# Zero matmuls ahead of a step: in the step's own PSUM tile, or in a spare tile first

## The chip, the cores and the metric

The kernel runs on one core of a Trainium2 chip. The metric is the device time of one execution in microseconds; lower is better. Three timed executions of the kernel before took 207.27, 207.66 and 207.92 us.

## The reference

A linear-attention recurrence (RWKV6) over 4 batches, 8 heads, 768 tokens and a head dimension of 48, followed by a gated feed-forward block (SwiGLU) on the 3072 tokens of width 384, with a hidden width of 1536. Inputs and output are float32.

```python
for t in range(S):
    cur = np.einsum('bhd,bhe->bhde', u[None] * kt, vt)
    y[:, :, t] = np.einsum('bhd,bhde->bhe', rt, state + cur)
    state = wt[:, :, :, None] * state + np.einsum('bhd,bhe->bhde', kt, vt)
...
xn = x / np.sqrt(np.mean(x * x, axis=-1, keepdims=True) + 1e-06) * rms_g
g = xn @ w_gate
out = (g * (1.0 / (1.0 + np.exp(-g))) * (xn @ w_val)) @ w_out
```

## The kernel before

The recurrence is worked in chunks of 128 tokens. There are six superblocks `n`, each with the chunks of the four batches `j`, and a step of the kernel carries its block as (n, j). For each chunk the kernel takes the logarithm of w (`ln`), sums it along the tokens by matmuls with a triangular mask (`cs_mm`), takes exponentials (`exp_r`, `exp_k`), scales r and k (`r_mul`, `k_mul`) and transposes both (`rk_pe` on TensorE and `rk_tr` as the copy out of PSUM, or `rk_tr` as a transposing DMA). It multiplies them (`q_mm`), masks the product (`q_mask_e` on VectorE for the even heads; `q_copy_o` and `q_mask_o` on ScalarE, GpSimd or VectorE for the odd ones), and forms the output of the chunk (`y_mm`) and the new state (`st_mm`, `st_new`). The bonus of the current token is worked on GpSimd and VectorE (`bonus_mul`, `bonus_sum`, `bonus_v`) and added in `x_add`. The normalized rows (`x_sq`, `x_rstd`, `xn_mul`) are transposed (`xn_pe` and `xn_out`, or `xn_tr`). The feed-forward block then runs over twelve column blocks `f` of the hidden width for each superblock: `gate_mm`, `silu`, `val_mm`, `h_mul`, and at last `o_mm`, `o_out` and `out_dma`.

The order of all steps is written out by hand in the table `ORDER`; each engine runs its instructions in that order. Loads and stores of the blocks are issued on the SP queue, the loads of the feed-forward weights on GpSimd's queue.

PSUM has eight tiles, in three rings: `a` and `b` with two each, `q` with four. A step that writes PSUM calls `psum(ring, key, shape)`, which picks the tile of the ring whose last user lies furthest back in the order, and opens a new tile under that tile's name. A new tile under a name waits until the tile before it under that name has been given back, that is until all who wrote or read it are done.

A number behind a colon in `ORDER` (`cs_mm.0.0:2`) asks for that many zero matmuls in front of the step; 17 entries have one, and the numbers add up to 50. The zero matmuls multiply the matrix `zero` (128 x 128, bf16) by itself, 384 columns at a time. Nobody reads what they write; they only keep TensorE working. They stand in `psum` at line 236, and go to a tile of their own under the same name (`spare`), which is given back before the step's tile is opened.

The entries with a number are:

```python
cs_mm.0.0:2 rk_pe.0.0:2 q_mm.0.0:4 q_mm.1.0:2 rk_pe.0.1:2 st_mm.0.1:4 cs_mm.0.3:3 q_mm.0.1:1 rk_pe.1.1:1
q_mm.1.1:7 y_mm.0.1:8 xn_pe.1.0:2 st_mm.1.1:3 rk_pe.0.3:3 val_mm.0.0:4 gate_mm.0.6:1 gate_mm.0.11:1
```

`rk_pe` and `xn_pe` open a bf16 tile, all the others a float32 tile.

Of the kernel before, what the change touches and what calls it, by code (L numbers as in the profile page):

```python
# [9 lines left out]
FP32 = mybir.dt.float32  # L10
BF16 = mybir.dt.bfloat16
# [7 lines left out]
def bc_mid(ap: bass.AP, n: int, axis: int = 1) -> bass.AP:  # L19
    new_ap = [list(x) for x in ap.ap]  # L20
    new_ap.insert(axis, [0, n])
    return dataclasses.replace(ap, ap=new_ap)
# [107 lines left out]
def kernel(  # L130
# [13 lines left out]
    nc = tc.nc  # L144
# [5 lines left out]
    DM = H * D  # L150
# [14 lines left out]
    psP = ctx.enter_context(tc.tile_pool(name="psP", bufs=1, space=bass.MemoryType.PSUM))  # L165
# [49 lines left out]
    steps, ahead = [], []  # L215
    for x in ORDER.split():
        x, _, m = x.partition(":")
# [3 lines left out]
    last_use, at = {}, [0]  # L221
# [6 lines left out]
    def psum(ring, key, shape, dtype=FP32):  # L228
        slots = rings[ring]
        k = min((x for x in range(len(slots)) if slots[x][0] < at[0]), key=lambda x: slots[x])  # L230
        taken[0] += 1
        slots[k] = [last_use.get(key, -1), taken[0]]
        if ahead[at[0]]:
            spare = psP.tile([128, 512], FP32, name="ps_" + ring + "uvxz"[k])
            for _ in range(ahead[at[0]]):
                nc.tensor.matmul(spare[:, 0:DM].rearrange("p (a x) -> p a x", a=3), lhsT=zero, rhs=bc_mid(zero, 3),
                                 start=True, stop=True)
            ahead[at[0]] = 0
        return psP.tile(shape, dtype, name="ps_" + ring + "uvxz"[k])

    table = [None]

# [45 lines left out]
    zero = const.tile([128, 128], BF16)  # L288
    nc.vector.memset(zero, 0.0)
    ident = const.tile([128, 128], BF16)  # L290
# [71 lines left out]
    def warm(n, j):  # L362
        ps = psum("q", ("warm", n, j), [128, DM])
        nc.tensor.matmul(ps.rearrange("p (a x) -> p a x", a=3), lhsT=zero, rhs=bc_mid(zero, 3), start=True, stop=True)

    def u_mm(n, j):
        ps = bank["u", n, j] = psum("q", ("u", n, j), [128, DM])
        nc.tensor.matmul(ps, lhsT=ones_row, rhs=u_row, start=True, stop=True)
# [4 lines left out]
    def g_mm(n, j):  # L373
        ps = bank["gain", n, j] = psum("q", ("gain", n, j), [128, KC])
        nc.tensor.matmul(ps, lhsT=g_row, rhs=i3, start=True, stop=True)
# [334 lines left out]
```

## Time and profile before

| | |
|---|---|
| timed runs | 207.27, 207.66, 207.92 us (median 207.66) |
| profiled execution | 206.26 us, of which 204.5 us are the span of the core's instructions |
| granted TensorE clock in the profile | 1.0 |
| zero matmuls | 50, in 17 groups, from 5.7 to 38.9 us |
| read from and written to memory | 25.96 MB and 4.72 MB |

The page of the profile names each group of instructions by line, engine, operation and tiles (`out<-in`). PE is TensorE's matmuls, PEld its weight loads, DVE VectorE, ACT ScalarE, POOL GpSimd and SP the queue that issues most DMAs. In a timeline a row is its start, its length, the engine, the line and the operation, how many instructions were merged into it (`x4`), and in brackets the idle time of the engine ahead of it with what ended it. The length of a merged row reaches from the first start to the last end. Matmuls overlap in the pipeline, so that the time from one start to the next can be much shorter than the length of one.

### The profile page before, as it was taken

Reading aid. Unit: us, or ns where it says so; the run is one execution under the profiler, and the core shown is the slowest. Engines: PE = TensorE matmul, PEld = TensorE weight load, DVE = VectorE, ACT = ScalarE, POOL = GpSimd, SP = SyncE. Lnnn points to the kernel's source line nnn. Section 1 sums busy time; section 2 is a strip of 40 time slices with the busy share of each in tenths; the row PEclk is TensorE's granted clock in tenths of the full one; section 3 lists DMA queues with packets and bytes.
Section 4 is the critical chain, followed back from the end, with each engine's and each line's share of the span. In section 5 each row is a group of like instructions: output and inputs, shape, how many; then the busy total and the mean of one; then the engine's idle time right before and its main releaser. Section 6 shows DMA issues by size and latency. Waiting matters only on the chain.

```text
span 204.5 us, 4563 instructions
## 1 busy us (share of the span) xinstructions
PE 193.3 (94%) x1657; PEld 120.9 (59%) x1674; DVE 157.8 (77%) x307; ACT 134.8 (66%) x278; POOL 124.4 (61%) x178
## 2 busy tenths in 40 slices
PE   1989999999999999999999998999999999999993
PEld 0355665465568998865556564656555555555562
DVE  5469879699998799998888997997989782225711
ACT  2625984769789666899658985899776683335310
POOL 6488958157849962689849555978699654200000
PEclk9999999999999999999999999999999999999999
DMA  6999999999989999969999999993465003030132
GB/s 148 240 231 221 172 206 203 193 203 180 195 174 227 184 172 239 196 144 148 201 227 203 227 221 158 206 213 77 136 180 106 0 19 101 0 115 0 65 111 98
DMA packets 121567, 32.42 MB, mean 159 GB/s; under 512 B 116420, under 2 KB 120392, under 8 KB 121544
## 3 DMA queue, kind: packets, MB, share of 16 engines
q1 hardware_dynamic: 119504, 28.58, 67.6%
q0 software_dynamic: 2032, 3.54, 9.9%
q8 instruction: 13, 0.21, 0.4%
q14 instruction: 10, 0.08, 0.1%
q10 hardware_dynamic: 8, 0.00, 0.0%
HBM read 25.96 MB, written 4.72 MB: 150 GB/s over the span
## 4 chain that ended last, share of the span: by engine, by line
PE 59%; DMA 4%; ACT 3%; DVE 2%; POOL 1%; SPq 1%; issue 1%; ACTq 0%; DVEq 0%; POOLq 0%
PE ps_qx L656 6%; PE ps_au L613 6%; PE ps_av L613 6%; PE ps_qv L656 6%; PE ps_bu L613 6%; PE ps_bv L613 5%; PE ps_qu L656 5%; PE ps_qz L656 4%; DMA rkT<-rk 2%; PE ps_au L618 2%; PE ps_bu L618 2%; DMA vt<-in_v_dram 2%; PE ps_av L618 2%; PE ps_bv L618 2%; ACT L245 1%
## 5 line engine op out<-in xcount | busy, mean ns | idle before, releaser
L656 PEld LDWEIGHTS <-ht 128*128 128x128 bf16 x300 | 28.1, 98 | 17.5 <-DVE ht L642 1.0
L247 ACT ACTIVATE sg<-ps_av 128x512 bf16<-128x512 f32 x36 | 21.5, 596 | 23.5 <-PE ps_av L613 18.4
L642 DVE TENSOR_TENSOR ht<-ps_bv,sg 128x512 bf16<-128x512 f32 x29 | 19.9, 685 | 13.9 <-PE ps_bv L613 13.0
L247 ACT ACTIVATE sg<-ps_au 128x512 bf16<-128x512 f32 x36 | 21.5, 596 | 11.9 <-PE ps_au L613 8.3
L613 PEld LDWEIGHTS <-wg_sb 128*128 128x128 bf16 x180 | 19.2, 114 | 16.7 <-issue 1.6
L613 PEld LDWEIGHTS <-wv_sb 128*128 128x128 bf16 x180 | 19.1, 114 | 15.9 <-issue 0.8
L471 POOL TENSOR_TENSOR ydiag<-vt,diag 128x384 f32<-128x384 f32 x24 | 20.0, 844 | 10.6 <-DVE diag L466 10.2
L461 POOL TENSOR_TENSOR ruk<-rt,kt 128x384 f32<-128x384 f32 x24 | 24.1, 1003 | 3.5 <-DMA kt<-in_k_dram 2.8
L613 PE MATMUL ps_av<-xnt,wg_sb 128*128 128x512 bf16 x88 | 25.0, 381 | 0.6 <-ACT sg L247 0.2
L642 DVE TENSOR_TENSOR ht<-ps_bu,sg 128x512 bf16<-128x512 f32 x31 | 21.2, 684 | 5.4 <-PE ps_bu L613 3.3
L462 POOL TENSOR_TENSOR ruk<-ruk,u_bc 128x384 f32<-128x384 f32 x24 | 24.0, 1000 | 1.9
L613 PE MATMUL ps_bu<-xnt,wv_sb 128*128 128x512 bf16 x86 | 24.8, 379 | 0.4
L613 PE MATMUL ps_au<-xnt,wg_sb 128*128 128x512 bf16 x87 | 23.6, 380 | 0.1
L613 PE MATMUL ps_bv<-xnt,wv_sb 128*128 128x512 bf16 x82 | 23.2, 380 | 0.3
L455 POOL TENSOR_TENSOR rk<-kt,ek 128x384 bf16<-128x384 f32 x16 | 15.9, 1001 | 9.9 <-ACT ek L247 5.7
L245 ACT ACT_TABLE_LOAD x14 | 18.0, 1283 | 1.9 <-PEq L694 1.6
L656 PE MATMUL ps_qx<-wo_sb,ht 128*128 128x384 bf16 x96 | 17.1, 326 | 0.2 <-DVE ht L642 0.2
L554 ACT ACTIVATE junk<-xb 128x384 bf16<-128x384 f32 x24 | 12.5, 520 | 5.2 <-DVE xb L549 5.1
L567 ACT ACTIVATE xn<-xb,rstd 128x384 bf16<-128x384 f32 x24 | 14.2, 609 | 1.1 <-POOL rstd L563 1.0
L466 DVE TENSOR_REDUCE diag<-ruk 128x8 f32<-128x384 f32 x24 | 12.9, 543 | 1.6 <-POOL ruk L462 1.6
L656 PE MATMUL ps_qv<-wo_sb,ht 128*128 128x384 bf16 (+1 forms) x84 | 13.8, 314 | 0.0
L247 ACT ACTIVATE lw<-wt 128x384 bf16<-128x384 f32 (+1 forms) x20 | 11.5, 582 | 2.3 <-DMA wt<-in_w_dram 2.3
(166 smaller groups left out, 407.3 us busy)
## 6 DMA issues: line engine op xcount, KB each, us to landing
rt<-in_r_dram SPq DMA_DIRECT2D x24, 192.0 KB, 3.9
vt<-in_v_dram SPq DMA_DIRECT2D x24, 192.0 KB, 4.0
kt<-in_k_dram SPq DMA_DIRECT2D x24, 192.0 KB, 4.0
out_dram<-ob SPq DMA_DIRECT2D x23, 192.0 KB, 2.2
wt<-in_w_dram SPq DMA_DIRECT2D x16, 192.0 KB, 4.1
wt<-in_w_dram SPq DMA_DIRECT2D x4, 384.0 KB, 4.2
wo_sb<-in_moe_w_out_dram POOLq DMA_DIRECT2D x3, 384.0 KB, 7.6
wg_sb<-in_moe_w_gate_dram POOLq DMA_DIRECT2D x1, 768.0 KB, 9.2
```

The lines of the kernel that those rows point to most:

```text
L245: nc.scalar.preload_act_table_set(table_name)
L247: return nc.scalar.activation(**kw).ins
L455: eng.tensor_tensor(out=rk[:, n % 2, j, 1, :, 0:D], in0=inp["k", n, j], in1=bank["cs_k", n, j][:, 0:DM].rearrange("p (h d) -> p h d", h=H) ...
L461: nc.gpsimd.tensor_tensor(out=ruk[n, j], in0=inp["r", n, j], in1=inp["k", n, j], op=ALU.mult)
L462: nc.gpsimd.tensor_tensor(out=ruk[n, j], in0=ruk[n, j], in1=u_bc, op=ALU.mult)
L466: nc.vector.tensor_reduce(out=diag[n, j].rearrange("p h o -> p (h o)"), in_=ruk[n, j], axis=mybir.AxisListType.X, op=ALU.add)
L471: nc.gpsimd.tensor_tensor(out=ydiag[n, j], in0=inp["v", n, j], in1=diag[n, j].to_broadcast([128, H, D]), op=ALU.mult)
L567: nc.scalar.activation(out=xn, in_=xb[n, j], func=AF.Copy, scale=rstd[n, j][:, 1:2])
L613: nc.tensor.matmul(ps, lhsT=units(ws, c, f), rhs=x[:, c, :], start=(c == 0), stop=(c == KC - 1))
L618: nc.tensor.matmul(ps[:, i * TS // 2:(i + 1) * TS // 2], lhsT=units(ws, c, f + i), rhs=x[:, c, cols], start=(i == 0 and c == 0), stop=(i = ...
L642: nc.vector.tensor_tensor(out=ht[n][:, f, :], in0=v, in1=sg, op=ALU.mult)
L656: nc.tensor.matmul(ps[:, cols], lhsT=ht[n][:, f, b * L:(b + 1) * L], rhs=wo_sb[:, f, cols], start=(f == 0), stop=(f == FC - 1))
```

## The change

The spare tile is gone. `psum` opens the step's own tile, writes the zero matmuls into that, and hands it to the step, whose first matmul starts a new sum and so overwrites them. In front of a bf16 tile each zero matmul becomes three transposes of `zero`, of 128 columns each. The numbers in `ORDER` and everything else stay. The changed file is four lines longer from there on, so a line L613 of the kernel before is L617 of the changed one.

```diff
         slots[k] = [last_use.get(key, -1), taken[0]]
-        if ahead[at[0]]:
-            spare = psP.tile([128, 512], FP32, name="ps_" + ring + "uvxz"[k])
-            for _ in range(ahead[at[0]]):
-                nc.tensor.matmul(spare[:, 0:DM].rearrange("p (a x) -> p a x", a=3), lhsT=zero, rhs=bc_mid(zero, 3),
+        ps = psP.tile(shape, dtype, name="ps_" + ring + "uvxz"[k])
+        flat = ps if len(shape) == 2 else ps.rearrange("p a b -> p (a b)")
+        for _ in range(ahead[at[0]]):
+            if dtype == BF16:
+                for c in range(3):
+                    nc.tensor.transpose(flat[:, c * 128:(c + 1) * 128], zero, ident)
+            else:
+                nc.tensor.matmul(flat[:, 0:DM].rearrange("p (a x) -> p a x", a=3), lhsT=zero, rhs=bc_mid(zero, 3),
                                  start=True, stop=True)
-            ahead[at[0]] = 0
-        return psP.tile(shape, dtype, name="ps_" + ring + "uvxz"[k])
+        ahead[at[0]] = 0
+        return ps
```

Only TensorE's instructions change; those of the other engines stand in the same order with the same waits. Two places show how. The first is PE at gate 6 of superblock 0 (`gate_mm.0.6:1`). Before (`zero` is the zero matrix, `wg_sb_127` the second part of the gate weights, and in brackets stands the engine that an instruction waits for):

```order
L236 LDWEIGHTS zero
L236 MATMUL ps_av<-zero 128x384 [waits Activation_49]
L613 LDWEIGHTS wg_sb_127
L613 MATMUL ps_av<-xnt,wg_sb_127 128x512 [waits PE_49]
L613 LDWEIGHTS wg_sb_127
L613 MATMUL ps_av<-xnt,wg_sb_127 128x512
```

After:

```order
L240 LDWEIGHTS zero
L240 MATMUL ps_av<-zero 128x384 [waits Activation_49]
L617 LDWEIGHTS wg_sb_127
L617 MATMUL ps_av<-xnt,wg_sb_127 128x512
L617 LDWEIGHTS wg_sb_127
L617 MATMUL ps_av<-xnt,wg_sb_127 128x512
```

The zero matmul keeps its wait for ScalarE, which frees the tile. The real matmul behind it has lost its wait for PE, which was the giving back of the spare tile.

The second place is PE at the transposes of r and k of block (1, 1) (`rk_pe.1.1:1`). Before (`rk` holds the scaled r and k, `ident` the identity):

```order
L236 LDWEIGHTS zero
L236 MATMUL ps_qu<-zero 128x384 [waits DVE_49]
L478 LDWEIGHTS rk
L478 MATMUL ps_qu<-ident,rk 128x128 [waits PE_49]
L478 LDWEIGHTS rk
```

After:

```order
L238 LDWEIGHTS zero
L238 MATMUL ps_qu<-ident,zero 128x128 [waits DVE_49]
L238 LDWEIGHTS zero
L238 MATMUL ps_qu<-ident,zero 128x128
L238 LDWEIGHTS zero
L238 MATMUL ps_qu<-ident,zero 128x128
L482 LDWEIGHTS rk
L482 MATMUL ps_qu<-ident,rk 128x128
```

One weight load and matmul have become three, and the wait for PE ahead of the first real transpose is gone. Ten of the 50 zero matmuls stand in front of bf16 tiles, so TensorE has 20 weight loads and 20 matmuls more. In the whole order 57 instructions of PE wait for PE before and 50 after: the 17 of the groups are gone, and ten have come up on matmuls that follow.

## The prediction

> **What bounds the kernel now.** I read the page first, then the instructions of the zero matmuls' line, the timeline of PE through the first 40 us, the stages by window, and the chain that ended last. Between the page's busy times and its slices, PE is the engine that is never free:
>
> ```profile
> PE 193.3 (94%) x1657; PEld 120.9 (59%) x1674; DVE 157.8 (77%) x307; ACT 134.8 (66%) x278; POOL 124.4 (61%) x178
> PE   1989999999999999999999998999999999999993
> DMA  6999999999989999969999999993465003030132
> ```
>
> The first line gives 94% of 204.5 us to PE; the second has 9 in nearly each slice after the first. The DMA engines are as full until slice 28, about 143 us. So work taken off PE is worth time where no load, and no other engine, ends the wait instead. The zero matmuls (L236) all lie in the first 40 us, in 17 groups:
>
> ```profile
> L236 PEld LDWEIGHTS <-zero x50: 95/98/147, 5.7 to 38.7; 128*128 128x128 bf16 x50
> L236 PE MATMUL ps_qv<-zero x16: 324/326/524, 9.6 to 29.3; 128*128 128x384 bf16 x16
> ```
>
> A zero matmul lasts 326 ns (524 in the first microseconds), but the next may start sooner. The 12 matmuls of 384 columns of an output step show the pace:
>
> ```profile
> 57.39 1.97 PE ps_qv L656 x12
> ```
>
> 1.97 / 12 = 0.16 us from start to start. Now three groups, each with the matmul that it stands in front of:
>
> ```profile
> 17.28 0.81 PE L236 MATMUL ps_qu<-zero 128*128 128x384 bf16 x4
> 18.15 0.34 PE L524 MATMUL ps_qu<-vb,rk 128*128 128x96 bf16 x4
> 37.92 0.33 PE L236 MATMUL ps_av<-zero 128*128 128x384 bf16 x1
> 38.30 0.81 PE L613 MATMUL ps_av<-xnt,wg_sb 128*128 128x512 bf16 x3
> 38.94 0.33 PE L236 MATMUL ps_au<-zero 128*128 128x384 bf16 x1
> 39.33 0.81 PE L613 MATMUL ps_au<-xnt,wg_sb 128*128 128x512 bf16 x3
> ```
>
> At 37.92 a single zero matmul starts and the real one starts at 38.30: 0.38 us, which is the 0.33 of the zero matmul and 0.05 more. PE waited for its own zero matmul to be complete, because the real tile takes the place of the spare one. Without that wait the pace of 0.16 would do: 0.38 - 0.16 = **0.22 us** a group. The group of four at 17.28 says the same (0.81 + 0.06 to 18.15).
>
> **The change part by part.** *The wait on PE itself.* The rows of gate 6 of superblock 0, under the change, show it for the group at 37.92. The wait for ACT, which frees the bank, stays on the zero matmul; the wait for PE is gone. That holds for all 17 groups. Ten waits for PE turn up on later matmuls that the old wait had covered, but they are for writers of the bank's previous step, long complete; I cost them at nothing, and at 0.22 us each if I misread that.
>
> *The zeros in bf16 tiles.* Ten of the 50 zero matmuls stand in front of transposes and become three transposes each. The rows of the transposes of block (1, 1), under the change, show one. Twenty weight loads and 20 matmuls more. What a transpose costs is in the eight real ones, once early and once later:
>
> ```profile
> 10.47 0.96 PE L478 MATMUL ps_qv<-ident,rk 128*128 128x128 bf16 x8
> 16.63 0.61 PE L478 MATMUL ps_qv<-ident,rk 128*128 128x128 bf16 x8
> ```
>
> With 0.22 us for the last one, (0.61 - 0.22) / 7 = 0.056 us each, so three are 0.17 us in place of 0.16: 10 x 0.01 = 0.1 us at the most, no term. No other engine's instructions move; DVE, ACT, POOL and SP have the same rows with the same waits.
>
> *What of 17 x 0.22 = 3.7 us reaches the end.* That is the outer bound. Where the real step waits for data anyway, a group gains nothing of its own, and up to 25 us two other engines cap what the rest gain:
>
> ```profile
> 14.90 0.23 PE L496 MATMUL ps_qx<-rkT 48*128 48x128 bf16 x1 [0.46 <-DVE rkT L485]
> 15.00:20.00 5.00, 4.82 (x62) 2.85 (x60) 5.00 (x12) 2.92 (x5) 4.02 (x6) 1.00 1.11 228
> 20.00:25.00 5.00, 4.82 (x54) 2.89 (x53) 4.10 (x8) 4.15 (x13) 4.77 (x7) 1.00 0.96 173
> 19.19 0.50 POOL L385 CAST vb<-vt 128x384 bf16<-128x384 f32 x1 [0.32 <-DMA vt<-in_v_dram]
> 23.52 1.48 PE L236 MATMUL ps_qv<-zero 128*128 128x384 bf16 x8
> 24.06 0.65 POOL L514 TENSOR_SCALAR_AFFINE_SELECT qts<-qts 128x512 bf16<-128x512 bf16 x1
> 25.05 0.36 PE L544 MATMUL ps_qv<-vb,qts 128*128 128x48 bf16 x8
> ```
>
> The first row is a group whose step waits 0.46 us for a copy of DVE (`rkT`); the second and third are windows of 5 us, with DVE busy for 5.00 and then POOL for 4.77. POOL's row at 19.19 is a cast that waited for its load, and from there POOL runs without a pause to its mask at 24.06, done at 24.71. The step behind the eight zero matmuls (25.05, `y_mm` of block (0, 1)) needs that mask from its second matmul on. So however early PE arrives, that matmul starts no sooner than about 24.8; it starts at about 25.05 now. Of the eleven groups up to here about **0.25 us** is left, whatever they save before.
>
> From 25 us on, PE itself sets the pace again:
>
> ```profile
> 26.03 0.48 PE L236 MATMUL ps_qz<-zero 128*128 128x384 bf16 x2
> 26.57 0.33 PE L582 MATMUL ps_qz<-ident,xn 128*128 128x128 bf16 x3
> 27.76 0.65 PE L236 MATMUL ps_qx<-zero 128*128 128x384 bf16 x3
> 28.46 0.33 PE L524 MATMUL ps_qx<-vb,rk 128*128 128x96 bf16 x4
> 27.81 0.61 ACT L567 ACTIVATE xn<-xb,rstd 128x384 bf16<-128x384 f32 x1 [0.24 <-POOL rstd L563]
> 28.80 0.33 PE L582 MATMUL ps_qz<-ident,xn 128*128 128x128 bf16 x3
> 28.96 0.65 PE L236 MATMUL ps_qv<-zero 128*128 128x384 bf16 x3
> 29.67 0.61 PE L478 MATMUL ps_qv<-ident,rk 128*128 128x128 bf16 x8
> 30.48 0.56 DVE L592 TENSOR_TENSOR xnt<-ps_qz,gT 128x384 bf16<-128x384 bf16 x1 [0.69 <-PE ps_qz L582]
> ```
>
> Three groups, 3 x 0.22 = 0.66. Between them the transposes at 28.80 read `xn`, which ACT ends at 27.81 + 0.61 = 28.42; with 0.05 for the signal that is 0.33 before PE needs it, and ACT's row hangs on the step at 25.05, which comes 0.25 earlier. So PE can be at most 0.33 + 0.25 = 0.58 earlier there, not 0.25 + 0.44 = 0.69: 0.1 is lost, and the three give about **0.55**. The fourth group of this stage (four zeros at 30.28) gains nothing of its own: its real step waits for DVE's row at 30.48, which waited 0.69 us for PE's transposes and comes earlier with them. The two gate groups at 37.92 and 38.94 add 2 x 0.22 = **0.44**, as the silus that free their banks wait for PE too. Sum at 39.3 us: 0.25 + 0.55 + 0.44 = **1.24 us**.
>
> *From there to the end.* No zero matmul is left, and PE is full, so what is won at 39.3 should arrive, less what another engine or a load keeps. The rows that speak of this:
>
> ```profile
> PE 59%; DMA 4%; ACT 3%; DVE 2%; POOL 1%; SPq 1%; issue 1%; ACTq 0%; DVEq 0%; POOLq 0%
> 55.89 0.66 PE L656 MATMUL ps_qx<-wo_sb,ht 128*128 128x384 bf16 x3 [0.18 <-DVE ht L642]
> 101.59 4.01 DMA vt<-in_v_dram
> 121.14 4.77 DMA rkT<-rk
> DMA to landing us min/median/max: 3.2/4.0/8.8
> ```
>
> The chain is PE for 59% of the span and holds two DMAs. At 55.89 PE waits 0.18 us for DVE, which follows PE's gates and so moves with them. Both DMAs are issued behind work of DVE and POOL, not by a clock of their own, so they move too; the last row is how long the loads of v took to land. I take 0.2 us off for the places where a load or a bank comes only when it came: 1.24 - 0.2 = **1.0 us**. Bounds: nothing (all taken by later waits), 2.0 on the other side (if the 25 us cap does not hold, about half of the first eleven groups' 2.4 come through).
>
> The profiled execution took 206.26 us, its span 204.5 and 1.8 around it; the sum makes 205.3 of it. The three timed runs have a median of 207.66, 1.4 above it, and I carry the 1.0 us over to that: **206.7 us**, 0.5% faster. 0.3%, or 0.62 us, is about what a measurement of this kernel can tell from no change.
>
> **The rivals.** *It is absorbed.* The 25 us cap is one example; between 40 and 140 us the DMA engines are as full as PE, and loads whose landing is set by the queue stop PE where it now arrives 1 us earlier. For it: the POOL row at 19.19 waits for a load, and the DMA row of the page shows no slack until 143 us. Against it: PE itself hardly ever waits (0.18 at 55.89). It would leave 0 to 0.5 us: 207.4.
>
> *The clock.* The matmuls are slow at first and then fast:
>
> ```profile
> 5.73 0.82 PE L236 MATMUL ps_au<-zero 128*128 128x384 bf16 x2
> 11.27 0.33 PE L524 MATMUL ps_qx<-vb,rk 128*128 128x96 bf16 x4
> ```
>
> Two zero matmuls take 0.82 us at 5.73 and two take 0.48 at 26.03; the eight transposes of 10.47 are still slow ((0.96 - 0.22) / 7 = 0.11 us each), the matmuls at 11.27 are not. In the changed kernel 0.6 us of zero matmuls just ahead of this, at 9.57, become transposes. If transposes do less to raise the clock, it rises later: what PE does from 11.27 to the end of the transposes at 13.95, 2.7 us, would at half pace take up to 2.7 us longer. I put it at half of this, 1.3, since the clock would rise within it. Of that the group of eight zeros at 23.52 and the waits around it take back a part, and the 1.0 us of the later groups comes off: about no change, 207.6. The Trainium skill, "TensorE: Matmul & The Clock Gate", Part 4: PE-mode transpose, says just this, that work in transpose mode does not count as PE-busy in the same way and does not bring the full clock. Against it stands that the clock rose while eight transposes ran; by the rule the time would be this rival's, not the forecast's. No run here has tried transposes alone.
>
> *The other side: a later landing.* The load of v at 101.59 lies on the chain (4.01 us to its landing; POOL's cast, ACT and PE wait behind it). With 1 us taken out of the work before it, SP issues it into another state of a queue that is full all through that stage. Loads of v took up to 8.8 us. It decides from a landing of 4.0 + 1.0 = 5.0 us on; half way from the median to the longest, 6.4, it would be 2.4 - 1.0 = 1.4 us slower: 209.1. The same holds for the transposing DMA of 4.77 at 121.14.
>
> **How the numbers follow.** Forecast (0.62 us or more gained) 0.50, with a range of its own from 205.7 to 207.0; absorbed 0.25, clock 0.08, both within 0.3%; a later landing 0.17. So faster 0.50, same 0.33, slower 0.17. The range goes from 2.0 us of gain, 205.7, to most of the way into the last rival, 208.6; the rest of it is left out.
>
> **What would show it.** Right: in the profile after, the real matmul behind the single zero matmul near 37 us starts 0.16 us after it, not 0.38; PE's rows at about 39.3 lie about 1.2 us earlier, those at 25.05 about 0.25; the span is 1.0 shorter. The cap is wrong if PE is much more than 0.3 us ahead at 25 us, the clock rival is right if matmuls after 11.3 still start 0.11 us apart, and a later landing would show as a DMA of over 5 us in the chain. The forecast fails if PE is 1.2 ahead at 39 us and the span is not shorter.

## The result and the profile after

The kernel after took 204.16 us (median of four runs, 203.96 to 204.62) beside 207.79 for the kernel before (207.27 to 208.08). The ratio is 0.9831, 95% interval 0.9804 to 0.9859: 3.6 us faster, where 1.0 was forecast. The profiled executions stand closer together: 206.26 us before, 203.96 after, 2.3 us. Three more comparisons of the same two kernels (below) gave ratios of 0.9898, 0.9890 and 0.9887. Medians here take in all runs and ratios leave out disturbed ones, so the one need not be the quotient of the other.

The page after, the line of busy times and the shares of the chain that ended last:

```profile
PE 191.3 (95%) x1677; PEld 121.9 (60%) x1694; DVE 157.5 (78%) x307; ACT 135.0 (67%) x278; POOL 124.4 (62%) x178
...
PE 65%; ACT 3%; DMA 2%; DVE 2%; issue 1%; SPq 0%; DVEq 0%; ACTq 0%
```

PE has 20 matmuls more, as said, and is busy 2.0 us less: a real matmul now starts while the last zero matmul is still in the pipeline, so that the two lengths overlap. In the chain PE's share has risen from 59% to 65%, and that of DMAs has fallen from 4% to 2%: one of the two DMAs that the prediction named is gone from it. PE's timeline after, at the places that the prediction spoke of:

```profile
9.34 0.84 PE L238 MATMUL ps_qv<-ident,zero 128*128 128x128 bf16 x6
9.98 0.70 PE L482 MATMUL ps_qv<-ident,rk 128*128 128x128 bf16 x8
10.52 0.33 PE L528 MATMUL ps_qx<-vb,rk 128*128 128x96 bf16 x4
...
24.68 0.35 PE L548 MATMUL ps_qv<-vb,qts 128*128 128x48 bf16 x7 [0.22 <-POOL qts L518]
...
29.40 0.81 PE L240 MATMUL ps_bv<-zero 128*128 128x384 bf16 x4
30.21 0.81 PE L617 MATMUL ps_bv<-xnt,wv_sb 128*128 128x512 bf16 x2
...
36.94 0.33 PE L240 MATMUL ps_av<-zero 128*128 128x384 bf16 x1
37.10 0.81 PE L617 MATMUL ps_av<-xnt,wg_sb 128*128 128x512 bf16 x3
37.74 0.33 PE L240 MATMUL ps_au<-zero 128*128 128x384 bf16 x1
37.91 0.81 PE L617 MATMUL ps_au<-xnt,wg_sb 128*128 128x512 bf16 x3
```

From 36.94 to 37.10 and from 37.74 to 37.91 it is 0.16 and 0.17 us, where it was 0.38 and 0.39. The real gate matmuls start at 37.10 and 37.91; they were at 38.30 and 39.33, so PE is 1.20 and then 1.42 us ahead. At 24.68 PE now waits for POOL's mask, as the cap of the prediction said.

DVE has the same 307 instructions in the same order in both kernels, so that one instruction's start can be set against the same one's. Four of them before:

```profile
25.44 0.56 DVE L549 TENSOR_TENSOR xb<-ps_qv,ydiag 128x384 f32<-128x384 f32 x1
...
41.99 0.69 DVE L642 TENSOR_TENSOR ht<-ps_bv,sg 128x512 bf16<-128x512 f32 x1 [0.20 <-PE ps_bv L613]
...
108.73 0.69 DVE L642 TENSOR_TENSOR ht<-ps_bu,sg 128x512 bf16<-128x512 f32 x1 [0.74 <-ACT sg L247]
...
126.61 0.69 DVE L503 TENSOR_TENSOR qts<-ps_qv,mask_lt 128x512 bf16<-128x512 f32 x1 [0.62 <-PE ps_qx L498]
```

The same four after:

```profile
25.07 0.56 DVE L553 TENSOR_TENSOR xb<-ps_qv,ydiag 128x384 f32<-128x384 f32 x1 [0.24 <-PE ps_qv L548]
...
40.58 0.69 DVE L646 TENSOR_TENSOR ht<-ps_bv,sg 128x512 bf16<-128x512 f32 x1 [0.20 <-PE ps_bv L617]
...
106.79 0.69 DVE L646 TENSOR_TENSOR ht<-ps_bu,sg 128x512 bf16<-128x512 f32 x1 [0.25 <-ACT sg L251]
...
124.50 0.69 DVE L507 TENSOR_TENSOR qts<-ps_qv,mask_lt 128x512 bf16<-128x512 f32 x1 [0.93 <-PE ps_qx L502]
```

The lead is 0.38 us, then 1.41, 1.94 and 2.11. The table gives it (start less that of the profile of before, in us) for these four and three more instructions, named by their starts before, in each profile used below:

| profile | 25.4 | 42.0 | 101.2 | 108.7 | 126.6 | 160.3 | 201.1 |
|---|---|---|---|---|---|---|---|
| after | -0.38 | -1.41 | -1.40 | -1.94 | -2.11 | -2.11 | -2.11 |
| e1, before again | 0.06 | 0.26 | 0.27 | 0.46 | 0.62 | 0.60 | 0.61 |
| e2, own tile late | 0.33 | -0.71 | -0.70 | -1.03 | -1.18 | -1.20 | -1.20 |
| e3, own tile early | 0.25 | 0.26 | 0.28 | 0.63 | 0.26 | 0.26 | 0.27 |
| e4, nine zeros at 38 us | 0.01 | 0.69 | 0.70 | 0.07 | 0.29 | 1.16 | 1.21 |
| e5, after again | -0.45 | -1.49 | -1.47 | -2.11 | -1.89 | -1.89 | -1.89 |
| e6, six zeros at 38 us | -0.61 | -0.67 | -0.65 | -1.29 | -0.60 | 0.29 | 0.34 |
| e7, late zeros out | -0.55 | -0.08 | -0.06 | -0.70 | -1.27 | -1.27 | -1.28 |
| e8, no zeros | -0.90 | -1.26 | -1.24 | -1.58 | -2.50 | -2.12 | -2.06 |
| e9, after again | -0.38 | -0.80 | -0.79 | -1.43 | -1.10 | -1.10 | -1.10 |
| e10, before, loads and store moved | -0.38 | -0.38 | -0.37 | -0.45 | 1.79 | 1.59 | 1.86 |
| e11, after, loads and store moved | 0.00 | -0.14 | -0.12 | -0.76 | 1.28 | 1.07 | 1.07 |
| e12, nine zeros at 174 us | -0.40 | -1.21 | -1.19 | -1.46 | -1.39 | -1.38 | 0.08 |
| e13, after again | 0.24 | 0.12 | 0.29 | 0.27 | 0.19 | 1.13 | 1.18 |
| e14, before, loads moved | -0.35 | -0.34 | -0.34 | 0.53 | 0.16 | 0.15 | 0.99 |
| e15, after, loads moved | -0.32 | -1.37 | -1.36 | -2.00 | -2.73 | -2.75 | -2.75 |
| e16, and two zeros less | 0.21 | -0.73 | -0.72 | -1.27 | -2.09 | -2.10 | -2.10 |

Between 42 and 101 us no row but e13's (0.17) changes by more than 0.02: what PE has won at 42 us nothing takes back there. What changes afterwards changes at single places, near 106, 125, 154 and 175 us, and there an engine waits for a DMA's landing, except at 175 us in e12, where zeros were added. Row e13 is the profile of an execution of 207.59 us; it is read below, with e13.

### The profile page after: what moved, and what is told of

Read it like the earlier page. It is cut to its first block, busy times and chain, and to the rows that moved or that the text cites. A ratio compares the mean times of both kernels' runs of the same rounds, so it can differ in the third digit from the quotient of the medians.

```text
span 202.2 us, 4604 instructions
## 1 busy us (share of the span) xinstructions
PE 191.3 (95%) x1677; PEld 121.9 (60%) x1694; DVE 157.5 (78%) x307; ACT 135.0 (67%) x278; POOL 124.4 (62%) x178
## 4 chain that ended last, share of the span: by engine, by line
PE 65%; ACT 3%; DMA 2%; DVE 2%; issue 1%; SPq 0%; DVEq 0%; ACTq 0%
PE ps_av L617 7%; PE ps_bu L617 7%; PE ps_au L617 7%; PE ps_bv L617 6%; PE ps_qx L660 6%; PE ps_qv L660 6%; PE ps_qu L660 5%; PE ps_qz L660 4%; PE ps_au L622 2%; PE ps_bu L622 2%; DMA rkT<-rk 2%; PE ps_av L622 2%; PE ps_bv L622 2%; ACT L249 1%; PE ps_au L419 1%; PE ps_qv L500 1%
## 5 line engine op out<-in xcount | busy, mean ns | idle before, releaser
L251 ACT ACTIVATE sg<-ps_au 128x512 bf16<-128x512 f32 x36 | 21.5, 596 | 11.5 <-PE ps_au L617 7.7
L617 PEld LDWEIGHTS <-wg_sb 128*128 128x128 bf16 x180 | 19.2, 114 | 15.9 <-issue 0.6
L617 PEld LDWEIGHTS <-wv_sb 128*128 128x128 bf16 x180 | 19.2, 114 | 15.7 <-issue 0.5
L617 PE MATMUL ps_av<-xnt,wg_sb 128*128 128x512 bf16 x88 | 25.0, 381 | 0.3
L617 PE MATMUL ps_bu<-xnt,wv_sb 128*128 128x512 bf16 x86 | 24.8, 380 | 0.4
L617 PE MATMUL ps_au<-xnt,wg_sb 128*128 128x512 bf16 x87 | 23.6, 380 | 0.1
L617 PE MATMUL ps_bv<-xnt,wv_sb 128*128 128x512 bf16 x82 | 23.2, 380 | 0.2
```

The lines of the kernel that those rows point to most:

```text
L251: return nc.scalar.activation(**kw).ins
L617: nc.tensor.matmul(ps, lhsT=units(ws, c, f), rhs=x[:, c, :], start=(c == 0), stop=(c == KC - 1))
```

## The experiments

Theories, as far as they go through all of these: W, the gain is the 1.4 us of PE's walk to 42 us and the rest is scatter between executions; L, landings of DMAs further on decide the rest; C, the moment at which the clock rises moves.

**e1: the kernel before, unchanged**, beside itself.

> The kernel before, unchanged, for a second profile. Its first profile took 206.3 us, while its timed runs had a median of 207.8. Theory L (the rest of the gain comes from loads that land sooner or later on the chain): the walk of PE up to 40 us is the same as in the first profile to 0.1 us, and the second profile differs, if it does, only behind DMA landings after 95 us. Theory C (the clock rises at another moment from run to run): the first 20 us differ, by up to 1.5 us. Time 207.7 by both, the profile between 206.2 and 208.

207.21 us (12 runs) beside 207.43 (29 runs, from 205.34 to 209.26); ratio 0.9984, 0.9949 to 1.0019. Two profiles of the same program differ by up to 0.6 us (table): 0.26 up to 42 us, not the 0.1 of theory L, and the rest at landings near 106 and 125. The clock rose sooner in this execution, at 10.08 us by the clock records of the trace against 11.25, and nothing of that is left at 25.4 us (0.06). Single executions scatter over 4 us. A profile is one draw from this, and so is a median of three or four.

**e2 and e3: one half of the change each.** In e2 only the six groups from `xn_pe.1.0` on write into the step's own tile, in e3 only the eleven before.

```diff
+        own = at[0] >= steps.index(("xn_pe", 1, 0))    # e3: <
+        if ahead[at[0]] and not own:
+            spare = psP.tile([128, 512], FP32, name="ps_" + ring + "uvxz"[k])
...
         ps = psP.tile(shape, dtype, name="ps_" + ring + "uvxz"[k])
```

> The step's own tile only for the six groups from xn_pe.1.0 on; the eleven before it keep the spare tile. By the walk of PE in the two traces the late groups bring 1.0 of the 1.4 us that PE is ahead at 39 us. Walk alone: 206.8. Theory L: the same 1.0 at 40 us, and the landings decide what is added, up to 1.5 more: 205.3 to 206.8. Theory C (the early, slow part decides): nothing beyond the 1.0: 206.8.

> The own tile only for the first eleven groups, the spare tile from xn_pe.1.0 on. Walk alone: 0.4 us at 25 us, carried to the end: 207.4. Theory C: the early stretch holds the part that the prediction missed, so 0.4 and 1.5 to 2 us more: about 205.7. Theory L: 207.4, or a jump of up to 0.7 where a landing falls differently.

e2: 205.89 us, ratio 0.9894 (0.9839 to 0.9948). e3: 206.86, ratio 0.9953 (0.9917 to 0.9990). In the table e2 gains 1.04 us between 25.4 and 42.0, as after does (1.03), and e3 gains nothing there. Before 25 us e3 is 0.89 us ahead at 11.5 us and has lost it again at 25.4, so the early groups' waits come back as other waits, as the prediction said, though the timed runs leave e3 about 1 us, more than its profile shows (as they do for e2: 2.2 us, and 1.2 in the profile). The late six carry most of the gain: theory C, which put it into the early stretch, missed in both.

**e4, e6 and e12: a hold of known size.** Zeros are added ahead of a gate step in the kernel after: nine at 38 us (1.46 us of PE), six there (0.98), and nine at 174 us.

```diff
-gate_mm.0.11:1
+gate_mm.0.11:10    (e6: :7)
...
-gate_mm.5.1
+gate_mm.5.1:9      (e12)
```

> The changed kernel with nine zero matmuls more in front of gate_mm.0.11, 9 x 0.16 = 1.46 us of PE at 38 us, which puts all that follows back to where it stood in the kernel before. Theory L: the landings after 40 us are then as before too, and the whole gain is gone: 207.5 to 207.8. Theory C: what was won early in the way of the clock stays, only the 1.46 goes: 205.6.

> The changed kernel with six zero matmuls more in front of gate_mm.0.11, 6 x 0.16 = 0.98 us of PE at 38 us. Theory W: 0.98 us above the changed kernel of the same chip. Theory L: more than that, 2 us, as nine of them took back the whole 3 us.

> The kernel after with 9 more zero matmuls (9 x 0.162 us = 1.46 us of PE) ahead of the first gate step of chunk 5 at 173.5 us, where PE is dense and no load is left to land. The same nine at 38 us made the kernel 3.0 us slower than the kernel after of another chip. Theory L: here exactly 1.4 to 1.5 us slower than after, since no landing behind it can add. Theory W says the same 1.4 to 1.5 us, and then the 3.0 was a difference of chips; a third (some slack at the end hides part of it) under 1.2.

e4: 207.39, ratio 1.0018 (0.9989 to 1.0047). e6: 205.98, 0.9983 (0.9955 to 1.0010), 1.6 us above the kernel after on its chip (e5). e12: 207.58, 0.9991 (0.9953 to 1.0029), 2.3 us above the kernel after on its chip (e9). The timed differences are too loose to tell 1.0 from 1.6, or 1.5 from 2.3, so the rows have to decide. The late hold in e12, on PE:

```profile
174.24 1.63 PE L240 MATMUL ps_av<-zero 128*128 128x384 bf16 x9
175.70 0.81 PE L617 MATMUL ps_av<-xnt,wg_sb 128*128 128x512 bf16 x2
```

It costs 1.46 us (174.24 to 175.70), and the table's last two columns say the same (-1.38 to 0.08): nothing is added where no load is left to land. The early hold in e4, and a place further on:

```profile
38.38 1.79 PE L240 MATMUL ps_au<-zero 128*128 128x384 bf16 x10
40.01 0.81 PE L617 MATMUL ps_au<-xnt,wg_sb 128*128 128x512 bf16 x3
...
154.59 0.23 PE L500 MATMUL ps_qz<-rkT 48*128 48x128 bf16 x1 [0.99 <-DMA rkT<-rk]
```

At 154.59 PE waits 0.99 us for a transpose that it did not wait for in the first profile of the kernel after; the transposing DMA issued at 150.12 took 4.42 us to land, against 2.78 and 2.79 in the profiles of after and before. e6 has the same wait (1.00 us, a landing of 4.37). So both executions with an early delay of PE paid for the delay and for a late landing. The landing is not the price of the delay alone, though: e13, the kernel after without any added zero, has the same wait in its profile. What else falls on that landing in all three is told in the next section, under the term that was wrong.

**e5, e9 and e13: the kernel after again**, on three chips.

> The changed kernel, unchanged, timed twelve times. The runs of the kernel before have turned out to scatter from 205.3 to 209.3 us around 207.4, so that four runs of each kernel say little of a single us. Theory W (the gain is what PE is ahead at 40 us, and the rest was scatter): 205.6 to 206.1, with runs up to 207. Theory L (the landings on the chain fall better in the changed kernel): it stays at 204.2 to 204.6, all runs below 205.5.

> The kernel after, unchanged, once more beside the kernel before, as the mark for the three runs with it. Theory L (PE is 1.4 us ahead at 40 us, and DMA landings on the chain between 100 and 126 us add some more, by what traffic stands beside them): 2.0 to 2.6 us faster than before. Theory W (1.4 us is all, and the rest of the 3.6 us was scatter between executions and chips): 1.2 to 1.8 us faster.

> The kernel after, unchanged, once more beside the kernel before. Theory L (1.4 us at 40 us and 0.5 to 1.0 at the landings near 104 and 124 us): 1.9 to 2.4 us faster than before. Theory S (the gain of the first comparison was real and the two later ones were low): 3 us or more. Theory W (1.4 us is all): 1.8 or less.

e5: 204.40 beside 206.23, ratio 0.9898 (0.9866 to 0.9929). e9: 205.25 beside 207.46, 0.9890 (0.9845 to 0.9936). e13: 205.35 beside 207.37, 0.9887 (0.9862 to 0.9912). That is 2.1 to 2.3 us three times, the 2.3 of the first two profiles. The first comparison lay at the upper end of the scatter; theory S, that the 3.6 was the true size, falls. The 1.4 us of the walk alone lie outside the intervals of e5 (from 1.5) and e13 (from 1.8), and just inside that of e9 (from 1.3).

e9 also shows a smaller gain up to 42 us (0.42 after 25.4, not 1.03). PE waited 0.32 us there for `xn`, and some 0.2 us for a gate weight that landed at 35.53. e11, below, has the second wait too, longer:

```profile
36.24 0.84 PE L617 MATMUL ps_av<-xnt,wg_sb 128*128 128x512 bf16 x3 [0.46 <-DMA wg_sb<-in_moe_w_gate_dram]
```

The kernel after reaches this step early enough that in some executions the weight has not landed: a new limit that the prediction's sum did not have.

The profile of e13 shows how much one execution can lose. Up to 40.5 us it gains as the others do (from 0.24 behind at 25.4 to 0.80 ahead). Then ScalarE waits for a load of v, PE waits for the silu behind that, and 0.92 us of the lead go at once; 1.1 us more go at 154 us:

```profile
39.48 0.51 ACT L387 CAST vb<-vt 128x384 bf16<-128x384 f32 x1 [1.31 <-DMA vt<-in_v_dram]
40.55 0.81 PE L617 MATMUL ps_av<-xnt,wg_sb 128*128 128x512 bf16 x2 [0.88 <-ACT sg L251]
...
154.57 0.23 PE L500 MATMUL ps_qz<-rkT 48*128 48x128 bf16 x1 [1.06 <-DMA rkT<-rk]
```

**e7 and e8: without the zeros.** e7 is the kernel after without the 14 zero matmuls of the six late groups, e8 without any.

```diff
-xn_pe.1.0:2 ... st_mm.1.1:3 ... rk_pe.0.3:3 ... val_mm.0.0:4 ... gate_mm.0.6:1 ... gate_mm.0.11:1
+xn_pe.1.0 ... st_mm.1.1 ... rk_pe.0.3 ... val_mm.0.0 ... gate_mm.0.6 ... gate_mm.0.11
```

> The changed kernel without the 14 zero matmuls from xn_pe.1.0 on (26 to 38 us): 14 x 0.16 = 2.3 us less for PE where PE sets the pace. Theory W: up to 2.3 us faster than the changed kernel, less what DVE or a load keeps, so 1 to 2 us. Theory L: not a matter of PE alone, anything from no change to 3 us.

> The changed kernel without any zero matmul, 50 x 0.16 = 8.1 us less for PE. If the zeros only take time: as much as the one without the late ones, or faster by up to 1 us, since up to 25 us other engines set the pace. If they are what raises the clock and keeps it up: the matmuls of 128 columns start 0.11 us apart for longer than to 11 us, and it is slower by 1 us or more.

e7: 204.49, ratio 0.9925 (0.9893 to 0.9956). e8: 204.25, 0.9907 (0.9880 to 0.9934). Both are within their intervals of e5. So theory W's 1 to 2 us for e7 missed, and so did the loss of 1 us or more that e8 had if the zeros were needed for the clock. What the zeros save and cost shows in e7's profile. The granted clock in 40 slices, from its page:

```profile
PEclk9999996999999999999999999999999999999999
```

PE's timeline in and ahead of the seventh slice (30.5 to 35.6 us):

```profile
28.18 0.34 PE L586 MATMUL ps_qz<-ident,xn 128*128 128x128 bf16 x3 [0.94 <-ACT xn L571]
...
30.24 1.09 PE L617 MATMUL ps_bv<-xnt,wv_sb 128*128 128x512 bf16 x2 [0.65 <-DVE xnt L596]
31.13 1.49 PE L617 MATMUL ps_au<-xnt,wg_sb 128*128 128x512 bf16 x3
32.41 1.49 PE L617 MATMUL ps_bu<-xnt,wv_sb 128*128 128x512 bf16 x3
...
34.24 0.84 PE L617 MATMUL ps_au<-xnt,wg_sb 128*128 128x512 bf16 x3
```

Without the zeros PE idles for 0.94 and 0.65 us, and the clock falls: it is 0.6 on average in that slice, and by the clock records of the trace 0.5 from 30.62 to 34.03. Three matmuls of 512 columns take 1.49 us and not 0.81, until 34 us. The zeros of `val_mm.0.0` filled exactly the wait for `xnt` (in the kernel after the real step starts at 30.21, here at 30.24). In e8 the clock falls likewise, to 0.5 from 23.71 to 30.54 us, around waits of 1.34 us (until 21.96) and 1.55 us (until 24.04). These zeros fill a wait, cost nothing and hold the clock: by the table e7 is 1.33 us behind after at 42 us and 0.83 at the end. The timed runs of e7 and e5 (204.49 and 204.40) don't show this difference. Without any zeros (e8) the early stretch is faster, and the lead at 42 us is almost that of after (1.26 against 1.41).

**e10 and e11: SP's queue reordered in both kernels.** Two loads and an output store come behind the two transposing DMAs of chunk 4.

```diff
-load_v.5.0 ... load_r.5.2 rk_tr.4.1 ... out_dma.2.1 ... load_k.4.2 rk_tr.4.0
+rk_tr.4.1 ... load_k.4.2 rk_tr.4.0 load_v.5.0 load_r.5.2 out_dma.2.1
```

> The kernel before with one reordering on SP's queue: two loads (v of pair 0 and r of pair 2, both of chunk 5) and one output store, which stand ahead of or between the DMA transposes of r and k for pairs 1 and 0 of chunk 4, come behind them. In the profile before, that second transpose took 4.77 us to land at 125.91, and PE waited 0.86 us for it; transposes at 148.84 and 150.17 with nothing beside them took 2.78. Theory L: the transpose lands in under 3.6 us, PE's wait at 126 us goes, and the run is 0.7 to 1.0 us faster than before. If landings there don't decide (theory W): within 0.4 us of before.

> The same reordering in the kernel after, where PE waits 0.59 us for that landing at 123.80. Theory L: 0.4 to 0.7 us faster than after, so that the two reordered kernels stand 1.4 to 2.0 us apart, which is the walk at 40 us (1.4) and the v landing at 104 us (0.5) and no more. Theory W: as fast as after, and as far from the reordered kernel before as after is from before.

e10: 208.80, ratio 1.0033 (1.0001 to 1.0066). e11: 207.09, 0.9983 (0.9952 to 1.0013), 1.8 us above e9. Both expectations missed, through the store. DVE in e11:

```profile
122.78 0.55 DVE L667 COPY ob<-ps_qv 128x384 f32<-128x384 f32 x1
126.36 0.56 DVE L667 COPY ob<-ps_qx 128x384 f32<-128x384 f32 x1 [3.03 <-DMA out_dram<-ob]
```

DVE's next copy needs the output buffer that this store empties, and waited 3.03 us for its landing (3.42 in e10). These two say nothing on the theory.

**e14, e15 and e16: the loads alone behind the transposes**, the store left in place; e16 also takes out the two single zeros ahead of gates 6 and 11.

```diff
-load_v.5.0 ... load_r.5.2 rk_tr.4.1 ... load_k.4.2 rk_tr.4.0
+rk_tr.4.1 ... load_k.4.2 rk_tr.4.0 load_v.5.0 load_r.5.2
...
-gate_mm.0.6:1 gate_mm.0.11:1    (e16)
+gate_mm.0.6 gate_mm.0.11
```

> The kernel before with the two loads (v of pair 0 and r of pair 2, chunk 5) behind the two DMA transposes of chunk 4, and the output store left where it was. Theory L: the store lands before it is waited for, the second transpose lands 1 to 1.5 us sooner than the 4.77 us of the first profile, PE's 0.86 us at 126 us goes, and the run is 0.6 to 0.9 us faster than before. If another wait takes that place: within 0.3 us of before.

> The same two loads moved in the kernel after, where PE waits 0.59 to 0.99 us for that transpose at 124 us. Theory L: 0.5 to 0.9 us faster than after, and 1.4 to 1.9 us faster than the kernel before with the same two loads moved. Without theory L: as far below it as after is below before.

> The kernel after with the two loads moved and without the two single zeros ahead of gate steps 6 and 11 at 37 and 38 us, where PE never idles: 2 x 0.16 = 0.32 us of PE less on the path. Expected 0.3 us faster than the kernel after with the loads moved alone, 0.8 to 1.2 faster than after. If the zeros are covered there, or the clock needs them: no faster than the loads alone.

e15: 203.80 (5 runs), ratio 0.9838 (0.9807 to 0.9868), against 0.9887 (0.9862 to 0.9912) for the kernel after beside it: 1.0 us faster by the ratios, whose intervals just touch, and below both kernels. PE in the kernel after, where it waits for the transpose:

```profile
122.44 0.81 PE L617 MATMUL ps_au<-xnt,wg_sb 128*128 128x512 bf16 x3
123.84 0.23 PE L500 MATMUL ps_qu<-rkT 48*128 48x128 bf16 x1 [0.59 <-DMA rkT<-rk]
```

And in e15:

```profile
122.48 0.81 PE L617 MATMUL ps_au<-xnt,wg_sb 128*128 128x512 bf16 x3
123.23 0.23 PE L500 MATMUL ps_qu<-rkT 48*128 48x128 bf16 x1
```

The wait of 0.59 us is gone and the lead grows by 0.62 there; from 25 us on nothing else differs by over 0.1. For this place theory L holds as stated.

e14: 207.11, ratio 1.0000 (0.9975 to 1.0025). Here the expectation missed: the transpose of the kernel before landed at 126.07 all the same, 5.2 us after its issue, PE still waited 0.48 us, and the profile loses 0.87 us near 106 to a load of v and 0.84 at 175 to a transposing DMA of `xnt`. So e14 and e15 stand 3.3 us apart and not 1.4 to 1.9. That a quieter queue alone brings the two kernels back to the walk's 1.4 us is refuted; which of them lands well depends on more than these two loads.

e16: 204.38, ratio 0.9855 (0.9821 to 0.9889), not distinguishable from e15. Its profile starts behind (0.53 us at 25.4, in loads and in the waits that follow) and gains 0.32 on e15 across the two gates: at their starts before, 35 to 48 us, the distance to e15 goes from 0.97 to 0.64. The two zeros were 0.32 us of PE's path as costed.

## Why the prediction was wrong in size

**Right: the wait on PE itself.** 0.38 against 0.16 us, 0.22 a group, measured as predicted. The ten waits that came up on later matmuls show nowhere, and neither does the pace of the transposes that replace zeros; what their 40 instructions more may do is told under the landings.

**Right: the cap at 25 us.** 0.38 us were left there, 0.25 forecast, and PE's row at 24.68 waits for POOL's mask. Copies of the kernel before differ by as much at that place (-0.38 to 0.06), and copies of the kernel after by more (-0.45 to 0.24), so the size of this term isn't measured well, only that it is small.

**Right: 25 to 42 us.** 0.55 + 0.44 = 0.99 was forecast; 1.03 came in the profile after, 1.04 in e5 and e2, 1.05 in e15. In e9 and e11 waits for `xn` and for a gate weight's landing took part of it, and in e13 a load of v took nearly all.

**Wrong: "I take 0.2 us off for the places where a load or a bank comes only when it came".** From 42 us on the profile shows 0.7 us more, not 0.2 less. 0.54 of it is at the load of v (between 101.2 and 108.7 in the table), the first of the two DMAs that the prediction named. Before, it was issued at 101.59, landed at 105.61, and stood on the chain; now the chain runs on PE through that stage:

```profile
103.65 0.65 PE ps_av L617 x3
104.30 0.17 PE ps_qv L528 x4
104.47 0.65 PE ps_bv L617 x3
...
120.13 3.66 DMA rkT<-rk
123.84 0.23 PE ps_qu L500
```

The load is issued at 99.47, 2.1 us earlier, though the engines were only 1.4 ahead, and takes 4.19 us, against 4.01 before: 0.72 of extra lead less 0.18 is the 0.54. SP's queue ran ahead of the engines because the transposing DMAs ahead of this load no longer held it up: the second of 90 us occupied SP for 2.19 us before and 1.24 after, the one issued next to last ahead of the load (98.68 before, 96.94 after) for 1.62 and 1.24; and the first of 90 us landed in 4.53 us before and 2.75 after (4.50 in e1, 2.75 in e5). The step that failed is "so they move too": that SP moves with the engines and no more. About the same 0.6 us stands in the table for e4, where PE was 0.7 us behind before at that point, so it isn't the lead as such. The other 0.17 is the transposing DMA of 121.14 us, 4.77 to land before and 3.66 after (4.45 in e1; 3.44 and 3.49 in e5 and e9). e15 shows this landing to be worth 0.62 us still.

What makes these transposes land sooner can be read from the DMA packets in the traces, though no run was made for it. Instructions are loaded by DMA as well, and the page counts the loads of 16 KB of one queue, 13 of them in both kernels and 12 in e8, which has 70 weight loads and 70 matmuls less than the kernel after:

```profile
q8 instruction: 13, 0.21, 0.4%
```

In the profile before, one such load begins for every 254 instructions of PE on average. The kernel after has 40 more of these (20 weight loads, 20 matmuls, all before 31 us), so that a load comes sooner in the order of the work. Before, one began at 92.1 us, 1.8 us after the first transpose of 90 us was issued; after, it began at 87.7, 1.2 us ahead of that. In seven of the 18 profiles (before, e1, e2, e3, e7, e10, e14) a load began while this transpose was on its way, and it landed in 4.22 to 4.56 us; in the other eleven none did, and it landed in 2.75 to 3.24. The seven have from 1670 to 1684 weight loads on PE, the others 1692 or more, or 1624 (e8). At the transpose of 121 us it is the same seven in which a load begins between 0.15 us ahead of its issue and 2.24 behind, and there it took 4.13 to 5.2 us; in the others whose landing the trace shows it took 3.16 to 3.78. At the second transpose of 150 us it is e4, e6 and e13, the three with the late landing; in the others the load begins 2.38 us behind the issue or later, or not at all, and changes nothing. So the prediction's "no term" for the 40 instructions is probably a term: they did not slow PE, but an instruction load moved off the transposes of 90 and 121 us. The two fall together at these three places without an exception; that the one delays the other is not shown by a run that moves an instruction load alone.

**Wrong: what the timed runs can tell.** "0.3%" was taken for the resolution. Single executions scatter over 4 us, medians of before in five comparisons stood from 206.2 to 207.8, and intervals from 5 to 12 runs were 0.25 to 0.55% to each side. The base, 207.66, was no bad one: four of the five medians lie between 207.3 and 207.8. Of the 3.6 us of the first comparison, 1.4 is the walk, 0.7 the landings in the profile, 0.2 the last store, which landed sooner behind the last copy, and about 1.3 (3.6 less 2.3) did not come again in three later comparisons; that part is scatter that happened to fall the same way. Even the 2.1 to 2.3 us that came again are more than the 2.0 that the prediction allowed on this side, because it let landings only take and never give.

**The rivals.** Absorbed: wrong between 42 and 101 us, where nothing was lost; right in kind at the gate weight of e9 and e11 and at the load of v in e13. A later landing: the two DMAs named did decide, but both in favour; e4, e6 and e13 show the rival's price at another landing, 1.0 us. The clock: the loss that this rival forecast did not come. In the profile after, the clock rose at 10.16 us, during the eight real transposes ((0.70 - 0.22) / 7 = 0.07 us each on average), and the matmuls at 10.52 are fast; before, it rose at 11.25. But that is no gain of the change either. By the clock records it rose between 9.94 and 11.25 us in the four profiles of the kernel before (before, e1, e10, e14; the later edits of e10 and e14 don't touch this stretch), and between 8.63 and 11.63 in the eleven that have the change and no other edit up to there (after, e4 to e7, e9, e11 to e13, e15, e16). The Trainium skill, "TensorE: Matmul & The Clock Gate", Part 4: PE-mode transpose, says that work in transpose mode does not bring the full clock. These runs don't decide it: in e9 and e13 all 14 transposes ran slow and the clock rose behind them, in after it rose during them, and in each of these kernels real matmuls had run since 6.7 us or sooner.

## What to carry to other kernels

A filler that shares its tile with the step behind it costs only its pace; one that gives a tile back first makes TensorE wait for its own completion, 0.22 us each time here. Walk such a gain to the next landing on the chain, and then ask of each queue on its own whether it moves with the engines: SP moved 2.1 us where they moved 1.4. Fillers are instructions too, and the loads of instructions moved with their number here. Take the scatter of the old kernel before stating what a measurement can tell, and set the sum against the execution it was made from.

## What the runs showed of the hardware

- The transposing DMAs of `rkT` landed 2.73 to 2.81 us after their issue in quiet stretches (2.78 and 2.79 at 148 to 150 us before), and up to 5.48 elsewhere (e3, 118.8 us); most of the differences between executions after 100 us arise where PE or DVE waits for one of them or for a load.
- Fifty zero matmuls, 8.1 us of PE at 0.162 each, can be left out without a measurable change (e8), and fourteen of them likewise (e7), though the granted clock then falls to 0.5, for 3.4 us in e7 and 6.8 in e8, where PE waits 0.65 to 1.55 us at a time.
- A delay at 38 us came back with 1.0 us on top at 154 us in two executions of two, but an execution without it had that wait too (e13, 1.06); the same delay at 174 us, with no load left to land, cost itself, 1.46.
- The granted clock rose to full at another moment in each execution: at 10.16, 9.78, 11.21 and 11.63 us in four of the kernel after (after, e5, e9, e13), at 11.25 and 10.08 in two of the kernel before. Of the 1.05 us between after and e9 nothing is left at 25.4 us (0.38 ahead in both).
- Of the 213 transposing DMAs of `rkT` whose landing the 18 traces show, 66 had an instruction load of 16 KB beginning while they were on their way and landed in 4.35 us (median); the other 147 landed in 2.80.
